# An attention and expert kernel: the issue order of its attention stage rewritten, and the combine's tail product given 128 columns of weights

## The chip, the core and the metric

The kernel runs on one core of one Trainium2 chip. The metric is the device time of one execution in microseconds (us); the kernel before takes 1121.13 us, the median of three runs (1117.65 to 1121.66). The core's engines run side by side and meet through semaphores: TensorE (PE for its matmuls, PEld for its weight loads), VectorE (DVE), ScalarE (ACT), GpSimd (POOL), and SyncE (SP), which here issues DMAs.

## The reference, cut to what matters

```
scores = 0.125 * q @ k.T                        # 4 batches, 8 heads, 576 tokens, 64 wide
keep   = scores >= rowmax(scores) - tau
attn   = softmax(where(keep, scores, -1e9))
x      = (attn @ v) as rows                     # [2304, 512]

logits = x @ w_gate                             # 8 experts, the best one per token
y      = p_best * (relu(x @ w1[e]) @ w2[e])     # e: the token's expert

out    = ((y @ wa) * (y @ wb)) @ wo             # inner width 1536
```

All inputs and the output are float32.

## The kernel before, in words

The work falls into three stages: attention with the gate (to about 415 us), the experts (to about 664 us), and the gated product with the stores of its rows. The change touches the first stage alone.

Attention works on 16 pairs of heads: pair i holds heads p and p+4 of batch i//4, with p = i % 4. A pair has nine score tiles: J, the joint last 64 tokens of both heads; A0 to A3, four blocks of 128 tokens of head a = 0; and B0 to B3 of a = 1. That makes 144 tiles g = 9i, 9i+1, and so on. One tile goes through five units. `s:g` is the score product on PE (line 644), into one of two PSUM buffers. `m:g` is the row maximum on DVE (line 657), `th:g` the threshold for two tiles at once (line 661), `e:g` the exponential on ACT (line 665). `p:g` is mask times exponential on DVE (line 677); it writes the tile P (J for the joint one) and is the last reader of the scores, so it frees the PSUM buffer for `s:g+2`. The units `J`, `C`, `H`, `A0` to `A3` and `B0` to `B3` transpose P on PE (line 752) into PSUM slots tp, tc, th and tj, and units that end in `e` and `l` bring each to SBUF as a high and a low part (pt and half; lines 702 to 717, on ACT, DVE or POOL). `v00` to `v11` are the products with v (line 824).

Ahead of a pair stand the splits of k, q and v into a high and a low part (`kh kl qh ql vh vl`, lines 392 and 406, on POOL from pair 1 on), their transposes on PE (`qk`, lines 432, 456 and 457), and the evacuations (`qe`).

Behind a pair, `x0` and `x1` are the combine for a = 0 and a = 1 (line 840 on): float32 products with the 72 columns W2 turn the transposed output o (64 + 8 columns wide by tokens) into rows, tx; four of them for the blocks of 128 tokens (line 851) and one for the 64 tokens of the tail (line 852). `x0s` and `x0t` scale them into x and xt (lines 857 and 866, DVE). Each float32 product is two passes with a weight load each.

After the last pair of a batch comes its gate (line 916 on): some two dozen small DVE instructions in a chain (sums of the logits L and lt, mx, val, first, oh, then ranks on PE, ex, cum, slot, si, base, g), the scaled rows xg and xh (lines 1004 and 1010), and the scatters. The gates of batches 0, 1 and 2 run amid the tiles of pairs 5, 9 and 13. `l_sel` is a chain of nine small DVE instructions behind the gate of batch 2 (lines 481 to 490) that picks the expert whose first rows are worked on early.

The order of all this is written out by hand: `ORDER` (line 59) is a string of 2713 unit names, and `emit` runs them one by one with the scheduler off. Each engine takes its instructions in that order; what one engine waits for is set by semaphores alone.

Of the kernel before, what the change touches and what calls it, by code (L numbers as in the profile page):

```python
# [23 lines left out]
H = 8  # L24
# [75 lines left out]
e:45 v10:3:2 p:44 qe:6:sk0 A1:4:3 A1:4:2 A1:4:0 A1:4:1 A0e:4 v10:3:3 p:45 s:46 v10:3:4 s:47 m:46 pj:45 A1e:4 A0l:4  # L100
A3:4:3 v10o:3 A3:4:2 A1l:4 A2:4:1 A2:4:0 e:46 z:40 A2:4:2 A2:4:3 A3:4:0 A3:4:1 v11:3:0 m:47 A2e:4 v11:3:1 v11:3:2
A3e:4 v11:3:3 th:47 A2l:4 v11:3:4 J2:4 p:46 e:47 qk:6:q0 H:4:1 s:48 qe:6:k2 A3l:4 H:4:0 H:4:2 v11o:3 qe:6:sk2 p:47
B0:4:1 B0:4:0 B0:4:2 m:48 qe:6:q0 s:49 kh:7 B0:4:3 x1:3 e:48 m:49 kl:7 v00:4:0 B0e:4 x1s:3 H:4:3 v00:4:1 v00:4:2
th:49 L:gate:3 v00:4:3 vh:6 e:49 p:48 qk:6:q1 B0l:4 He:4 p:49 s:50 qe:6:q1 Hl:4 s:51 qh:7 m:50 B1:4:3 B1:4:2 B1:4:0
ql:7 B1:4:1 v00:4:4 m:51 B1e:4 B2:4:0 B2:4:2 B2:4:3 B2:4:1 e:50 B1l:4 vl:6 lk:8 v00o:4 th:51 x1t:3 B3:4:0 p:50 e:51
B3:4:1 B3:4:3 v01:4:0 v01:4:1 v01:4:2 B2e:4 lt:gate:3 p:51 v01:4:3 lv:7 tl:gate:3 v01:4:4 B2l:4 s:52 top:gate:3
v01o:4 s:53 C:5:0 shift:gate:3 B3:4:2 tr:gate:3 m:52 ex:gate:3 v10:4:0 Ce:5 B3e:4 v10:4:1 slot:gate:3 v10:4:2 e:52
J:5:0 B3l:4 J:5:1 J:5:2 J:5:3 base:gate:3 gate:3 g:gate:3 Je:5 qk:7:t m:53 qe:7:kt x0:4 qe:7:t xg1:gate:3 xg2:gate:3
e:53 v10:4:3 qk:7:k0 sc1:gate:3 v10:4:4 xg0:gate:3 qe:7:k0 v10o:4 A0:5:3 sc2:gate:3 xh:gate:3 A0:5:0 A0:5:2 A0:5:1
A0e:5 sc0:gate:3 th:53 Cl:5 p:52 A1:5:1 A1:5:3 A1:5:2 sc4:gate:3 A1:5:0 qk:7:k2 p:53 A1e:5 s:54 qe:7:k2 xg3:gate:3  # L110
A1l:5 s:55 m:54 A2:5:3 A2:5:0 A2:5:2 A2:5:1 m:55 A3:5:1 A3:5:0 e:54 A3:5:2 A3:5:3 sc3:gate:3 qe:7:sk2 v11:4:0 rinv:4
v11:4:1 e:55 v11:4:2 th:55 x0s:4 v11:4:3 p:54 v11:4:4 A2e:5 Jl:5 A3e:5 p:55 s:56 kh:8 x0t:4 s:57 A2l:5 v11o:4 A3l:5
qe:7:sk0 H:5:3 H:5:0 m:56 H:5:1 H:5:2 qk:7:q0 He:5 B0:5:3 m:57 B0:5:1 B0:5:2 B0:5:0 kl:8 e:56 Hl:5 e:57 th:57 x1:4
p:56 pj:54 qe:7:q0 J2:5 p:57 s:58 B0e:5 qk:7:q1 x1s:4 A0l:5 s:59 m:58 qe:7:q1 B1:5:3 B1:5:2 B1:5:0 m:59 B1:5:1 e:58
# [134 lines left out]
class Attention:  # L249
# [1482 lines left out]
```

## Time and profile before

| what | us |
|---|---|
| median of 3 runs | 1121.13 |
| lowest and highest run | 1117.65, 1121.66 |
| the profiled execution | 1126.54 |
| its span | 1124.8 |
| PE busy in the span | 1056.7 |
| DVE busy | 801.7 |
| POOL busy | 686.5 |
| ACT busy | 503.9 |

The profiled execution took 1126.54 us, of which 1124.8 are the span from the first to the last recorded instruction. Its mean granted TensorE clock was 0.98 of 2.4 GHz. Busy time of one engine says nothing yet on what another waits for; for that the stage has to be cut into stretches.

### The profile page before, as it was taken

What the parts mean: (1) busy time and instruction counts of PE and PEld (TensorE: products, weight loads), DVE (VectorE), ACT (ScalarE), POOL (GpSimd) and SP (SyncE); (2) the same over time, 40 slices, a digit from 0 to 9 for tenths busy, and PEclk for the clock granted to TensorE, in tenths of its full rate; (3) what the DMA queues carried; (4) which work ended last, traced back from release to release, by engine and by line L of the source; (5) the groups of instructions that cost most, each with busy time, mean ns of one, the idle gap of its engine ahead of it and who ended that gap; (6) DMA issues with size and microseconds to landing.
All of it is one profiled execution on the core that took longest, in us unless ns stands there. A gap on an engine that the chain in (4) does not pass through costs nothing. (4 is left out here: it accounts for less than half of the span.)

```text
span 1124.8 us, 19277 instructions
## 1 busy us (share of the span) xinstructions
PE 1056.7 (94%) x6492; PEld 947.7 (84%) x6492; DVE 801.7 (71%) x1765; ACT 503.9 (45%) x1047; POOL 686.5 (61%) x720
## 2 busy tenths in 40 slices
PE   3899989989988989999999979999999999999996
PEld 3799889979978979999999968888888888888885
DVE  4888888898888787644445799597496794984212
ACT  3788768867856533333334433442231321322110
POOL 3779798888886646555567846455364563654234
PEclk9899999999989998999999989999999999999999
DMA  4478632233222258545556522121011110110012
GB/s 128 116 208 243 188 97 67 77 96 84 69 75 66 86 160 277 174 147 150 159 162 199 161 65 65 49 74 39 20 57 39 38 56 20 57 39 1 10 66 93
DMA packets 105558, 111.81 MB, mean 99 GB/s; under 512 B 16704, under 2 KB 79168, under 8 KB 105456
## 3 DMA queue, kind: packets, MB, share of 16 engines
q1 hardware_dynamic: 101502, 100.79, 31.0%
q0 software_dynamic: 3552, 9.45, 2.2%
q8 instruction: 53, 0.87, 0.3%
q14 instruction: 49, 0.40, 0.1%
q10 hardware_dynamic: 402, 0.29, 0.1%
HBM read 77.47 MB, written 23.08 MB: 89 GB/s over the span
## 5 line engine op out<-in xcount | busy, mean ns | idle before, releaser
L1621 PE MATMUL pg<-y,w 128*128 128x512 f32 (+1 forms) x1440 | 308.6, 373 | 6.5 <-DVEq L1555 6.5
L1621 PEld LDWEIGHTS pg<-y,w 128*128 128x128 f32 x1440 | 253.0, 189 | 58.4 <-ACTq L1555 6.7
L1631 POOL TENSOR_TENSOR g<-gg,g 128x512 fp32r<-128x512 f32 (+1 forms) x60 | 73.3, 1222 | 138.9 <-ACT g L1630 131.4
L1644 PE MATMUL po<-w,g 128*128 128x512 f32 x648 | 152.7, 391 | 0.0
L1644 PEld LDWEIGHTS po<-w,g 128*128 128x128 f32 x648 | 121.2, 188 | 26.2
L717 POOL TENSOR_TENSOR pt<-st,pt 128x512 fp32r<-128x512 f32 x93 | 119.7, 1289 | 28.7 <-ACT pt L707 17.0
L1455 PE MATMUL ph_i<-xt_i,w 128*128 128x256 f32 (+5 forms) x768 | 124.7, 312 | 2.7 <-ACT w L1367 1.7
L1472 PE MATMUL py_i<-h_i,w 128*128 128x256 f32 (+5 forms) x768 | 119.9, 305 | 3.2 <-DVE h_i L1459 1.9
L1455 PEld LDWEIGHTS ph_i<-xt_i,w 128*128 128x128 f32 x768 | 113.2, 191 | 4.2 <-ACT w L1367 1.9
L1472 PEld LDWEIGHTS py_i<-h_i,w 128*128 128x128 f32 x768 | 111.7, 188 | 4.0 <-DVE h_i L1459 2.3
L1628 DVE TENSOR_TENSOR gg<-ga,pg 128x512 f32<-128x512 f32 (+1 forms) x60 | 37.8, 630 | 103.7 <-PE pg L1621 97.3
L1368 DVE TENSOR_TENSOR w<-raw,w 128x512 fp32r<-128x512 f32 x64 | 63.1, 988 | 60.7 <-ACT w L1367 59.3
L1370 POOL TENSOR_SCALAR w<-raw 128x512 fp32r<-128x512 f32 x64 | 50.9, 797 | 86.5 <-DMA raw<-in_moe_w 57.1
L1630 ACT CAST g<-gg 128x512 fp32r<-128x512 f32 (+1 forms) x60 | 34.6, 576 | 149.2 <-DVE gg L1628 79.6
L1401 POOL TENSOR_TENSOR t<-t,w 128x256 f32<-128x256 f32 x72 | 63.7, 890 | 57.8 <-DVE u L1397 26.5
L824 PE MATMUL pv<-pt,sv 128*128 128x288 f32 x512 | 97.4, 313 | 0.8 <-POOL pt L717 0.6
L1371 POOL TENSOR_TENSOR w<-raw,w 128x512 fp32r<-128x512 f32 x64 | 89.3, 1396 | 4.8
L752 PE MATMUL tp<-idf,P 128*128 128x128 f32 x504 | 82.3, 281 | 4.6 <-ACT pt L707 1.5
L1649 DVE TENSOR_TENSOR acc<-acc,po 128x512 f32<-128x512 f32 x90 | 60.5, 683 | 26.8 <-PE po L1644 26.8
L824 PEld LDWEIGHTS pv<-pt,sv 128*128 128x128 f32 x512 | 74.0, 191 | 2.5 <-POOL pt L717 0.8
L1400 POOL TENSOR_TENSOR mag<-a,u 128x256 f32<-128x256 f32 x72 | 60.6, 842 | 24.2 <-DVE a L1398 24.2
L1391 ACT ACTIVATE mag<-raw 128x256 f32<-128x256 f32 x72 | 31.2, 437 | 95.3 <-DVE w L1402 95.2
(267 smaller groups left out, 2079.4 us busy)
## 6 DMA issues: line engine op xcount, KB each, us to landing
raw<-in_moe_w SPq DMA_DIRECT2D x128, 256.0 KB
xs<-zero SPq DMA_DIRECT2D x16, 768.0 KB
raw<-in_moe_w_a SPq DMA_DIRECT2D x12, 512.0 KB
raw<-in_moe_w_b SPq DMA_DIRECT2D x12, 512.0 KB
raw<-in_moe_w_out SPq DMA_DIRECT2D x12, 512.0 KB
kT<-kT SPq DMA_DIRECT2D x32, 160.0 KB
kT<-kT SPq DMA_DIRECT2D x32, 144.0 KB
raw_k<-in_k SPq DMA_DIRECT2D x16, 256.0 KB
```

The lines of the kernel that those rows point to most:

```text
L717: nc.gpsimd.tensor_sub(lo, st, fr(hi))
L752: nc.tensor.transpose(st["ps"][:, 128 * j:128 * j + 128], parts(j), idf)
L824: nc.tensor.matmul(R["v", n][:, 0:HALF], lhs, rhs[r], start=(c == 0 and r == 0), stop=(c == 4 and r == 1))
L1368: nc.vector.tensor_sub(lo_t, raw, fr(hi_t))
L1371: self.last_pool = nc.gpsimd.tensor_sub(lo_t, raw, fr(hi_t)).ins
L1400: g.tensor_sub(mag, a.bitcast(F32), u.bitcast(F32))
L1401: g.tensor_sub(t, t, fr(hi))
L1455: nc.tensor.matmul(ps[:, 0:n], w[a][:, k, :], xt[b][:, k, 0:n], start=(s_ == 0), stop=(s_ == len(steps) - 1))
L1472: nc.tensor.matmul(st["y"][d][:, 0:n], w[a][:, 0, d * P:d * P + P], h[b][:, 0:n], start=(f == 0 and (a, b) == (0, 0)), stop=(f == 7 and a ...
L1621: nc.tensor.matmul(ps[:, 0:n], w[g][j][m][a][:, k, :], self.y[b][:, k, c0:c0 + n], start=(s_ == 0), stop=(s_ == len(steps) - 1))
L1631: last = nc.gpsimd.tensor_sub(gl[:, 0:n], gt[:, 0:n], fr(gh)[:, 0:n])
L1644: nc.tensor.matmul(ps, res[j][a][:, t * P:t * P + P], w[g][j][2][b][:, 0, :], start=(s_ == 0), stop=(s_ == len(steps) - 1))
```

## The change: a new order, and a wider tail product

There are two edits. The first is the text of `ORDER`: the same 2713 units in another order, so that no unit is added or taken away. The order of the experts and of the gated stage is as it was. One line of the new table, amid the gate of batch 2, against the one nearest to it in the old:

```diff
-v10:12:3 v10:12:4 base:gate:11 gate:11 qe:15:t g:gate:11 x0:12 A0e:13 th:125 xg2:gate:11 xg1:gate:11 qk:15:k0
+g:gate:11 v01:12:1 v01:12:2 e:123 B3l:12 th:123 v01:12:3 xg2:gate:11 v01:12:4 p:122 tr:gate:11 v01o:12 A1:13:3
```

The second is in the combine:

```diff
-            ot = (0, 512)[a]
+            ot = (0, 448)[a]
...
-                nc.tensor.matmul(pv_[64 * a:64 * a + 64, 4, :], o[:, ot:ot + 64], w2, start=True, stop=True)
+                nc.tensor.matmul(pv_[:, 4, :], o[:, ot:ot + 128], w2, start=True, stop=True)
```

The weights of the tail's product are now 128 columns of o instead of 64. For a = 0 they are tokens 0 to 127 of o, whose first 64 are the tail; for a = 1 the last 128, whose last 64 are the tail. The result fills all 128 partitions of its 72 columns, and `x0t` and `x1t` read the same 64 of them as before. Lines behind 841 move down by one.

What the new order moves is shown at three places; the numbers behind names only tell one tile from another.

The first place is the start. On POOL, the splits of q (sq1) and k (sk1) of pair 1, before:

```order
L392 TENSOR_SCALAR sq1_276<-raw_q1_242 128x9x64
L406 TENSOR_TENSOR sq1_276<-raw_q1_242,sq1_276 128x9x64
L392 TENSOR_SCALAR sk1_298<-raw_k1_239 128x9x64
L406 TENSOR_TENSOR sk1_298<-raw_k1_239,sk1_298 128x9x64
L392 TENSOR_SCALAR sk2_364<-raw_k2_303 128x9x64
L406 TENSOR_TENSOR sk2_364<-raw_k2_303,sk2_364 128x9x64
```

and now:

```order
L392 TENSOR_SCALAR sk1_289<-raw_k1_239 128x9x64
L406 TENSOR_TENSOR sk1_289<-raw_k1_239,sk1_289 128x9x64
L392 TENSOR_SCALAR sq1_298<-raw_q1_242 128x9x64
L406 TENSOR_TENSOR sq1_298<-raw_q1_242,sq1_298 128x9x64
L392 TENSOR_SCALAR sk2_358<-raw_k2_304 128x9x64
L406 TENSOR_TENSOR sk2_358<-raw_k2_304,sk2_358 128x9x64
```

The k of pair 1 is split ahead of its q; the four instructions are the same.

On PE at the same place, the transposes of pair 1 (tt1, tq1) and the first score products (S0_J0, S0_A0), before:

```order
L456 MATMUL tt1_313<-idr_67,sq1_276 128x128
L457 MATMUL tt1_313<-idr_67,sk1_298 128x128
L432 MATMUL tq1_316<-idr_67,sq1_276 128x128 x4
L432 MATMUL tq1_324<-idr_67,sq1_276 128x128 x4
L432 MATMUL tq1_330<-idr_67,sk1_298 128x128 x4
L644 MATMUL S0_J0_335<-kT0_267,qj0_245 128x288 x8
```

and now:

```order
L456 MATMUL tt1_313<-idr_67,sq1_298 128x128
L457 MATMUL tt1_313<-idr_67,sk1_289 128x128
L432 MATMUL tq1_317<-idr_67,sk1_289 128x128 x4
L432 MATMUL tq1_322<-idr_67,sq1_298 128x128 x4
L644 MATMUL S0_J0_331<-kT0_273,qj0_245 128x288 x8
L644 MATMUL S0_A0_340<-kT0_273,qT0_276 128x288 x4
```

Two groups of four transposes of pair 1 stand ahead of the first score product instead of three; the other two follow behind S0_A0, where one did before.

The second place is the gate of batch 2, on DVE, amid the tiles B0 to B3 of pair 13 (P13_0 to P13_3 are their `p` units, mt their maxima). Before, the last rows ahead of P13_2; P13_1 stands 13 rows above the first of them:

```order
L985 TENSOR_REDUCE slot_70<-cum2_4761 128x5
L987 CAST si2_4765<-slot_70 128x4
L989 TENSOR_SCALAR si2_4765<-slot_70,role_203 128x1
L993 TENSOR_TENSOR base_71<-base_71,tr2_4749 128x8
L975 TENSOR_REDUCE g2_4780<-ex2_4744 128x5
L976 TENSOR_SCALAR g2_4780<-g2_4780 128x5
L977 RECIPROCAL g2_4780<-g2_4780 128x5
L661 TENSOR_REDUCE m13_B2_4733<-mt2_213 128x2
L1004 TENSOR_SCALAR xg2_4794<-x2_3517,g2_4780 128x512
L1010 TENSOR_SCALAR xh2_4802<-xt2_3518,g2_4780 128x256
L1004 TENSOR_SCALAR xg2_4794<-x2_3517,g2_4780 128x512
L677 SCALAR_TENSOR_TENSOR P13_2_4613,sg1_227<-S13_B2_4694,m13_B2_4733,e13_B2_4759 128x576
```

and now, from P13_0 on:

```order
L677 SCALAR_TENSOR_TENSOR P13_0_4551,sg1_227<-S13_B0_4623,m13_B0_4650,e13_B0_4656 128x576
L983 TENSOR_TENSOR cum2_4728<-tr2_4716,base_71 128x40
L984 TENSOR_TENSOR cum2_4728<-cum2_4728,oh_69 128x40
L986 TENSOR_REDUCE slot_70<-cum2_4728 128x5
L988 CAST si2_4732<-slot_70 128x4
L990 TENSOR_SCALAR si2_4732<-slot_70,role_203 128x1
L677 SCALAR_TENSOR_TENSOR P13_1_4561,sg1_227<-S13_B1_4645,m13_B0_4650,e13_B1_4704 128x576
L994 TENSOR_TENSOR base_71<-base_71,tr2_4716 128x8
L1011 TENSOR_SCALAR xh2_4767<-xt2_3521,g2_4696 128x256
L657 TENSOR_REDUCE mt2_213<-S13_B2_4742 128x1
L657 TENSOR_REDUCE mt2_213<-S13_B3_4770 128x1
L711 TENSOR_TENSOR half1_13_4758<-tc13_4753,half0_13_4757 128x2x64
```

The gate's chain no longer stands in one piece between P13_1 and P13_2: the rows from mx to g stand ahead of P13_0, those from cum to si between P13_0 and P13_1, base and xh behind P13_1.

The third place is `l_sel`, on DVE. Before, it stands between the tiles P14_0 and P14_1 of pair 14:

```order
L677 SCALAR_TENSOR_TENSOR P14_0_4911,sg2_229<-S14_A0_4856,m14_J0_4854,e14_A0_4888 128x576
L711 TENSOR_TENSOR half1_13_4700<-th13_4882,half0_13_4699 128x512
L481 TENSOR_TENSOR l_cnt_4929<-base_71,eb_85 128x8
L483 TENSOR_REDUCE l_mx_4931<-l_cnt_4929 128x1
L484 TENSOR_SCALAR l_cnt_4929<-l_cnt_4929,l_mx_4931 128x8
L485 TENSOR_TENSOR l_cnt_4929<-l_cnt_4929,desc_190 128x8
L486 TENSOR_REDUCE l_mx_4931<-l_cnt_4929 128x1
L487 TENSOR_SCALAR sel_72<-l_cnt_4929,l_mx_4931 128x8
L488 TENSOR_SCALAR kept_73<-l_mx_4931 128x1
L489 TENSOR_SCALAR l_mx_4931<-l_mx_4931 128x1
L490 CAST lead_74<-l_mx_4931 128x1
L657 TENSOR_REDUCE mt4_219<-S14_A1_4913 128x1
```

and now:

```order
L677 SCALAR_TENSOR_TENSOR P13_2_4614,sg1_227<-S13_B2_4742,m13_B2_4788,e13_B2_4812 128x576
L1005 TENSOR_SCALAR xg2_4711<-x2_3520,g2_4696 128x512
L481 TENSOR_TENSOR l_cnt_4845<-base_71,eb_85 128x8
L483 TENSOR_REDUCE l_mx_4847<-l_cnt_4845 128x1
L484 TENSOR_SCALAR l_cnt_4845<-l_cnt_4845,l_mx_4847 128x8
L485 TENSOR_TENSOR l_cnt_4845<-l_cnt_4845,desc_190 128x8
L486 TENSOR_REDUCE l_mx_4847<-l_cnt_4845 128x1
L487 TENSOR_SCALAR sel_72<-l_cnt_4845,l_mx_4847 128x8
L488 TENSOR_SCALAR kept_73<-l_mx_4847 128x1
L489 TENSOR_SCALAR l_mx_4847<-l_mx_4847 128x1
L490 CAST lead_74<-l_mx_4847 128x1
L657 TENSOR_REDUCE mt3_216<-S14_J0_4833 128x1
```

It stands between P13_2 and P13_3 (three rows below the last one shown), directly behind the gate of batch 2.

## Rows read from the trace of the kernel before

**Rows 1.** Busy time by stretch: window, length, busy us of PE, PEld, DVE, ACT, POOL, PEclk, DMA, GB/s

```profile
40.00:130.00 90.00, 87.38 (x675) 81.59 (x673) 79.43 (x184) 73.92 (x147) 72.31 (x79) 0.99 0.74 213
130.00:150.00 20.00, 16.21 (x117) 14.47 (x117) 16.48 (x47) 11.60 (x25) 15.74 (x16) 0.94 0.31 97
...
230.00:250.00 20.00, 16.73 (x127) 14.28 (x126) 17.87 (x47) 14.41 (x29) 17.06 (x20) 1.00 0.29 91
...
315.00:345.00 30.00, 23.38 (x159) 21.26 (x158) 26.14 (x68) 17.16 (x35) 22.02 (x24) 0.84 0.20 64
```

**Rows 2.** Waits of PE, 0 to 430 us: total us, times, longest us

```profile
PE S_A L644 <- DVE P L677: 5.9, 10, 2.2
...
PE S_B L644 <- DVE P L677: 5.1, 10, 1.7
```

**Rows 3.** Timeline, 8 to 21 us: start, us, engine, line, operation, names, [idle before]

```profile
8.96 0.56 SPq L372 DMA_DIRECT2D raw_k<-in_k  x1
...
10.07 0.56 SPq L372 DMA_DIRECT2D raw_q<-in_q  x1
...
14.61 0.67 POOL L392 TENSOR_SCALAR sq<-raw_q 128x576 fp32r<-128x576 f32 x1 [12.20 <-DMA raw_q<-in_q]
...
20.12 0.71 PE L432 MATMUL tq<-idr,sk 128*128 128x128 f32 x4
...
20.62 2.25 PE L644 MATMUL S_J<-kT,qj 128*128 128x288 f32 x8
```

**Rows 4.** Timeline of PE at one combine

```profile
128.78 1.01 PE L851 MATMUL tx<-W,o 128*128 128x72 f32 x8
...
129.72 0.34 PE L852 MATMUL tx<-W,o 128*64 128x72 f32 x2
...
129.99 0.54 PE L824 MATMUL pv<-pt,sv 128*128 128x288 f32 x2
```

**Rows 5.** Weight loads of the combine's products, 0 to 425 us: busy us, mean ns

```profile
L851 PEld LDWEIGHTS tx<-W,o 128*128 128x128 f32 x256 | 32.1, 195 | 3.6 <-issue 2.1 <-DVE half L711 1.1 <-ACT qT L450 0.2
...
L852 PEld LDWEIGHTS tx<-W,o 128*64 128x64 f32 x64 | 6.2, 137 | 2.4
```

**Rows 6.** Timeline of DVE: P around the gates of batches 0, 1, 2

```profile
136.71 0.81 DVE L677 SCALAR_TENSOR_TENSOR P<-S_B,m_B,e_B 128x576 f32<-128x576 f32 x1
...
144.75 0.80 DVE L677 SCALAR_TENSOR_TENSOR P<-S_B,m_B,e_B 128x576 f32<-128x576 f32 x1
...
227.00 0.81 DVE L677 SCALAR_TENSOR_TENSOR P<-S_B,m_B,e_B 128x576 f32<-128x576 f32 x1
...
236.32 0.81 DVE L677 SCALAR_TENSOR_TENSOR P<-S_B,m_B,e_B 128x576 f32<-128x576 f32 x1
...
315.49 0.81 DVE L677 SCALAR_TENSOR_TENSOR P<-S_B,m_B,e_B 128x576 f32<-128x576 f32 x1
...
321.51 0.18 DVE L982 TENSOR_TENSOR cum<-tr,base 128x40 f32<-128x40 f32 x1
...
322.46 0.19 DVE L975 TENSOR_REDUCE g<-ex 128x5 f32<-128x40 f32 x1
...
323.52 0.79 DVE L1010 TENSOR_SCALAR xh<-xt,g 128x256 f32<-128x256 f32 x1
...
325.06 0.80 DVE L677 SCALAR_TENSOR_TENSOR P<-S_B,m_B,e_B 128x576 f32<-128x576 f32 x1
```

**Rows 7.** Groups of DVE, 0 to 425 us: busy us, mean ns

```profile
L711 DVE TENSOR_TENSOR pt<-tp,pt 128x512 fp32r<-128x512 f32 x33 | 22.5, 683 | 0.1
```

**Rows 8.** Timeline of DVE around l_sel

```profile
333.09 0.81 DVE L677 SCALAR_TENSOR_TENSOR P<-S_A,m_J,e_A 128x576 f32<-128x576 f32 x1
...
334.43 0.39 DVE L481 TENSOR_TENSOR l_cnt<-base,eb 128x8 f32<-128x8 f32 x1
...
338.39 1.41 DVE L657 TENSOR_REDUCE mt<-S_A 128x1 f32<-128x576 f32 x2
...
340.25 0.82 DVE L677 SCALAR_TENSOR_TENSOR P<-S_A,m_A,e_A 128x576 f32<-128x576 f32 x1
```

More of the change, by code (lines that the diff above doesn't have):

```diff
@@ L100 @@
[L100 to L114, printed above, removed]
@@ L220 @@
[L220 to L222 removed]
+kh:0 qh:0 ql:0 kl:0 qk:0:t qk:0:q1 qe:0:t qk:0:k2 qe:0:kt qe:0:q1 qk:0:k0 qe:0:k2 qk:0:q0 kh:1 qe:0:k0 qe:0:sk2
+qe:0:q0 kl:1 qe:0:sk0 qh:1 vh:0 vl:0 ql:1 lk:2 lv:1 qk:1:t qe:1:t qk:1:k0 qk:1:q0 qe:1:kt qe:1:k0 s:0 s:1 m:0
@@ new lines @@
+slot:gate:3 Je:5 e:49 x0:4 g:gate:3 th:49 xg3:gate:3 xg2:gate:3 sc3:gate:3 p:48 base:gate:3 gate:3 s:50 xh:gate:3
+xg1:gate:3 p:49 kh:7 m:50 kl:7 A0:5:2 v10:4:0 v10:4:1 A0:5:0 v10:4:2 A0:5:1 s:51 rinv:4 A0:5:3 e:50 m:51 qh:7 A0e:5
+Cl:5 th:51 p:50 v10:4:3 v10:4:4 sc1:gate:3 e:51 A1:5:0 A1:5:2 xg0:gate:3 s:52 sc4:gate:3 v10o:4 A1:5:1 p:51 A1:5:3
+A3:5:0 sc0:gate:3 m:52 A1e:5 A3:5:1 A3:5:2 s:53 x0s:4 e:52 ql:7 A1l:5 A2:5:0 A2:5:2 A2:5:1 m:53 A2:5:3 A3:5:3 A2e:5
+v11:4:0 lk:8 x0t:4 v11:4:1 th:53 qk:7:t e:53 p:52 v11:4:2 v11:4:3 qe:7:t A0l:5 v11:4:4 p:53 s:54 qe:7:kt A3e:5 A2l:5
@@ new lines @@
+lt:gate:7 v00:8:3 m:86 tl:gate:7 B1:8:0 B2:8:3 B2:8:1 B0l:8 B1e:8 B2:8:0 top:gate:7 lv:11 v00:8:4 C:9:0 B2:8:2 e:86
+m:87 v00o:8 J2:8 Ce:9 shift:gate:7 v01:8:0 B2e:8 th:87 v01:8:1 B1l:8 v01:8:2 e:87 B2l:8 tr:gate:7 p:86 v01:8:3
+ex:gate:7 B3:8:3 B3:8:0 B3:8:2 slot:gate:7 B3:8:1 s:88 B3e:8 v01:8:4 base:gate:7 gate:7 p:87 J:9:0 B3l:8 J:9:1
+v01o:8 J:9:3 qk:11:t J:9:2 m:88 s:89 qe:11:t Cl:9 e:88 g:gate:7 x0:8 m:89 xg3:gate:7 qe:11:kt Je:9 xh:gate:7
+xg1:gate:7 qk:11:k0 e:89 v10:8:0 v10:8:1 xg2:gate:7 sc3:gate:7 A0:9:2 A0:9:3 qe:11:k0 A0:9:1 A0:9:0 xg0:gate:7
@@ new lines @@
+xg1:gate:11 v10:12:2 base:gate:11 gate:11 xh:gate:11 qe:15:t s:125 sc1:gate:11 qk:15:k0 qe:15:kt v10:12:3 m:124
+qe:15:k0 v10:12:4 sc4:gate:11 A0:13:1 A0:13:2 A0:13:0 m:125 A0:13:3 v10o:12 x0:12 qe:15:sk0 e:124 Cl:13 sc2:gate:11
+th:125 e:125 A1l:13 A2:13:3 A2:13:0 A2:13:1 A2:13:2 A0e:13 p:124 xg0:gate:11 s:126 sc3:gate:11 l_sel qk:15:k2
+sc0:gate:11 A2e:13 v11:12:0 qe:15:k2 v11:12:1 v11:12:2 m:126 v11:12:3 qe:15:sk2 A3:13:2 A3:13:1 A0l:13 x0s:12
+A3:13:0 v11:12:4 e:126 A3:13:3 x0t:12 p:125 H:13:2 A3e:13 H:13:1 H:13:0 vh:15 A2l:13 H:13:3 s:127 He:13 A3l:13
@@ new lines @@
+x1t:15 L:gate:15 l_wd:5:0 l_wl:5:1 l_ah:1 l_wh:5:1 lt:gate:15 l_ad:1 l_b:0 l_wd:5:1 l_wl:6:0 tl:gate:15 l_ap:2
+top:gate:15 shift:gate:15 tr:gate:15 ex:gate:15 l_wh:6:0 g:gate:15 slot:gate:15 l_ah:2 xg3:gate:15 xg2:gate:15
+sc3:gate:15 l_ad:2 l_b:1 l_ap:3 xg0:gate:15 l_wd:6:0 l_wl:6:1 xg1:gate:15 xh:gate:15 sc0:gate:15 l_ah:3 base:gate:15
+gate:15 sc4:gate:15 l_ad:3 l_b:2 l_ap:4 sc1:gate:15 l_wh:6:1 l_ah:4 sc2:gate:15 l_ad:4 l_b:3 l_ap:5 l_wd:6:1 l_ah:5
+l_ad:5 l_b:4 l_ap:6 l_wl:7:0 l_wh:7:0 l_wd:7:0 l_wl:7:1 l_wh:7:1 l_wd:7:1 l_ah:6 l_ad:6 l_b:5 l_ap:7 l_ah:7 l_ad:7
```

287 lines of the change are left out of this document (140 added, 147 removed).

## The prediction

> **What bounds the kernel now.** I read the table of busy shares first, then busy time by stretch, then PE's waits, then the timeline at the places where PE waits. Over the whole span PE is busy 94% (the table in the section on time and profile), so only two things can move the time: less work for PE, or less idle time of PE. By stretch the second is seen to be uneven. In an undisturbed stretch of attention, 40 to 130 us, PE is busy for 87.38 of 90 us and DVE for 79.43 [rows 1]: PE is the bound there, and DVE has 10.6 us to spare. In the three stretches with a gate PE is busy for 16.21 of 20, 16.73 of 20 and 23.38 of 30 us [rows 1], so it lacks 3.8, 3.3 and 6.6 us; DVE has 16.48, 17.87 and 26.14 there, and in the first two it sits in a chain of small dependent instructions. At the share of the undisturbed stretch (97.1%) the three together would lack 2.0 us in their 70, so 3.8 + 3.3 + 6.6 − 2.0 = 11.7 us of idle time are extra. The third also has a mean granted clock of 0.84 and the first of 0.94 [rows 1]. There are two levels, 2.4 and 1.2 GHz; if the missing share is time at 1.2 GHz, full speed is missed for 0.16 × 30 + 0.06 × 20 = 6.0 us. Extra idle time and clock together are 17.7 us, an upper bound of what the gates cost.
>
> PE's own waits say for what: the score products of A and B tiles wait for a P of DVE 20 times, 5.9 + 5.1 = 11.0 us in all [rows 2]. The reason is in the two PSUM buffers of the scores: P is the last reader, so a gap between two P's on DVE is a gap between two score products on PE, and PE lives through it only on transposes and products with v that are ready by then.
>
> **The start.** POOL waits 12.20 us for raw_q before it splits q of pair 1 at 14.61 [rows 3], and the k of pair 1 is split behind it. The issue of raw_k stands at 8.96, that of raw_q at 10.07 [rows 3]. With k first, POOL can start by the 1.1 us between the two issues earlier, if k lands as much earlier as it is issued; that is an estimate from the issues. PE's transposes of pair 1 wait for both splits, whose sum is the same, so they come 1.1 us earlier. Then one group of four transposes less stands ahead of the first score product: 20.12 to 20.62 is 0.5 us [rows 3]. Everything behind depends on this first score, and PE has nothing else: −1.1 − 0.5 = −1.6 us. Bounds: if both transfers land together, only the 0.5 stays, and if the group that was put off is in the way of S0_A1, nothing; no reason is seen for a loss, but the same four transposes placed later could cost their 0.5 again: +0.5 to −1.7.
>
> **The tail product.** It is issued 32 times, two passes each. Eight passes with 128 columns of weights run from 128.78 to 129.72, 0.94 us, so 0.235 for a product of two; the tail's two passes with 64 columns run from 129.72 to 129.99, 0.27 us [rows 4]. With 128 columns it is one more product like the four before it: 32 × (0.235 − 0.27) = −1.1 us, all of it on PE, which is the bound. What speaks against it is the weight load: the loads take 195 ns with 128 columns, 137 ns with 64 [rows 5]. Each is under the matmul before it as long as that one is longer. If it were not, 64 × 0.058 = +3.7 us would come in place of the gain. I take −1.1, since a product of this very form stands four times next to the one that is replaced; the ends are −1.1 and +3.7. DVE waits for tx afterwards as before.
>
> The Trainium skill has a rule that speaks against this edit: in "TensorE: Matmul & The Clock Gate", section "LDWEIGHTS (loading the stationary operand)", the time of a weight load goes by the number of columns alone, so twice the columns would be twice the load. By it the loads would grow by 64 × 0.137 = 8.8 us and, if nothing hid them, the time to 1121.13 − 1.6 − 4.1 + 8.8 = 1124.2 us. The trace agrees in direction but not in size (195 against 137 ns is 1.42 times, not 2) [rows 5], and it shows that the product with the wider load is no longer one [rows 4].
>
> **The gates.** Before, DVE's gate stands in one lump between two P's. The gaps from P to P are 136.71 to 144.75 = 8.04 us, 227.00 to 236.32 = 9.32 us, and 315.49 to 325.06 = 9.57 us [rows 6]. In the new order P's stand amid the chain (the second excerpt of the order). Priced on batch 2: the rows cum to base leave the long lump, 321.51 to 322.46 = −0.95; xh and the xg behind it leave it too, 323.52 to 325.06 = −1.54 [rows 6]. An evacuation pt (line 711) comes into it, +0.68 [rows 7], and the small sum lt, for which I take the 0.19 of the reduction g [rows 6]. Together −1.6. In batch 1 the same pieces are spread over three gaps, and I take −1.6 as well; in batch 0 xh, the other xg and base fall behind the next P and one pt comes in, −1.54 + 0.68 = −0.9. Sum −4.1 us. I count it in full, because in these gaps PE runs dry: it is idle there beyond the share of the quiet stretch. What is taken out of a lump is work that DVE must still do; it falls among P's where DVE has its 10.6 us in 90 to spare, which is what hides it. The bounds: 0, if the total of DVE over a gate's stretch decides and not its longest lump (17.87 of 20 us is near to that), and −9, half of the 17.7 us, if the split lets PE go on through most of each gate.
>
> **The lead select.** The gap with l_sel runs from the P at 333.09 to the P at 340.25, 7.16 us, of which 334.43 to 338.39 = 3.96 is l_sel itself [rows 8]. In its new place the gap holds the same 3.96 beside an xg, one mt, an x and an xt (third excerpt of the order and the three rows behind it), where it held an evacuation half, two mt and three small rows before; about as much work, so I count 0 for the gap alone. What is different is its place: right behind the gate of batch 2 instead of 8 us later. It is the third rival.
>
> The rest of the order, among quiet tiles, is counted as 0: PE has 97% there, and the new order can neither gain more than the 2.6 us in 90 nor is a reason seen for a loss. The end of attention keeps its chain: last gate, lead expert, first expert weights.
>
> **The sum.** −1.6 − 1.1 − 4.1 = −6.8 us. Against the profiled execution: 1126.54 − 6.8 = 1119.7 us, with 1.7 us of it outside the span as before. That execution stands 5.4 us above the median of the runs (1121.13), so the forecast for the median is 1121.13 − 6.8 = 1114.3 us. Its own range is 1110 to 1118.
>
> **The rivals.** First, the gates stay bound by DVE's total: what is cut from one gap is given back in the next. For it speaks DVE's 17.87 of 20 us in the gate of batch 1; against it, 16.48 of 20 in that of batch 0 [rows 1]. Left are the start and the tail: 1121.13 − 2.7 = 1118.4 us.
>
> Second, the gates lose half of what they cost: −1.6 − 1.1 − 9 = −11.7, 1109.4 us. For it speaks that a chain split among P's leaves no P waiting for more than a few small instructions; against it, that a P is also late when its maximum is.
>
> Third, on the other side: the gate of batch 2 and l_sel become one lump. Before, 8.03 us (325.06 to 333.09) lie between the two gaps [rows 6, 8], in which PE works off what was held up. In the new order only P13_1 and P13_2 lie between them. If PE is dry by then, l_sel's 3.96 us come in full, and PE stays idle long enough to fall to 1.2 GHz once more, which in this stretch costs its 0.16 × 30 = 4.8 us again: +8.8. With the other gates as in the first rival that is 1121.13 − 2.7 + 8.8 = 1127.2 us, 1123 to 1132 by how much of it comes. Against it speaks that xg and the maxima are fewer in this lump. It decides from the point at which the same tiles lose over 8.3 us more than the 6.6 idle and 4.8 of clock they lose now, some 19.7 us.
>
> Fourth, the weight load is not hidden: 1121.13 − 1.6 + 3.7 − 4.1 = 1119.1 us.
>
> **How the numbers follow.** Forecast 0.36, first rival 0.22, second 0.13, third 0.24, fourth 0.05. About 0.5%, or 5.6 us, is what a measurement of this kernel can tell from no change, so faster is below 1115.5 and slower above 1126.7. Faster: 0.30 of the forecast, all of the second, 0.02 of the first: 0.45. Slower: 0.17 of the third and 0.02 for the unknown: 0.19. The same: 0.36. The range is 1105 to 1127: it leaves out about the upper half of the third rival and a little below the second.
>
> **What the profile after would show.** The start is right if the first S_J begins near 19.0 instead of 20.62. The tail is right if its product takes about 0.235 us next to the four others, and wrong if PE's idle time before it grows. The gates are right if the longest gaps between P's fall to about 7 to 8 us and PE's idle time in the three gate stretches falls by about as much; if the gaps fall and the idle time does not, it is the first rival. The third shows as a longer dry stretch of PE from P13_1 to P14_1, with a granted clock of 1.2 GHz over more than 10 us. What would make the whole prediction wrong is a loss in the quiet stretches, with PE under 97%, where I saw no reason for one.

## The result, and the profile after

The changed kernel takes 1111.01 us (median of five runs, 1107.43 to 1112.53); the kernel before, on the same chip, 1121.13 us (1117.65 to 1129.03). The ratio is 0.989, with a 95% interval of 0.987 to 0.991. By the medians that is 10 us less, by the ratio 12, where 6.8 were forecast.

The two profiled executions lie further apart, with spans of 1124.8 and 1105.7 us: the one of before is 5.4 us above its kernel's median, the one of after (1107.43) 3.6 below. About half of the 19 us is thus the luck of two executions, so a single profile is not enough for a gain in time.

Nearly all of it lies ahead of the experts: their first product on PE starts at 414.7 us before and at 396.7 after, 18.0 us apart. For a comparison tile by tile, the stretches below are cut at the masks P of tiles 8, 44, 62, 80, 116 and 143; the gates of batches 0, 1 and 2 lie in the third, fifth and sixth. The windows of the kernel before (length; busy us of PE, PEld, DVE, ACT and POOL; PEclk, the mean granted TensorE clock as a share of 2.4 GHz; DMA share, GB/s; the last line is the whole):

```profile
0.00:41.66 41.66, 19.86 (x114) 18.08 (x115) 23.49 (x88) 18.42 (x37) 19.66 (x34) 0.92 0.46 118
41.66:121.28 79.62, 77.32 (x603) 72.28 (x603) 70.83 (x167) 65.69 (x131) 64.11 (x70) 1.00 0.73 208
121.28:170.41 49.13, 44.15 (x328) 40.37 (x328) 42.33 (x107) 34.51 (x70) 41.98 (x45) 0.97 0.41 124
170.41:211.57 41.16, 39.74 (x313) 37.45 (x313) 36.64 (x86) 34.56 (x68) 35.30 (x39) 1.00 0.26 67
211.57:299.88 88.31, 83.57 (x648) 76.70 (x647) 79.38 (x192) 69.29 (x137) 76.75 (x83) 1.00 0.31 86
299.88:376.03 76.15, 68.03 (x504) 63.49 (x502) 66.90 (x162) 53.52 (x104) 55.55 (x61) 0.93 0.21 64
376.03:414.70 38.67, 35.01 (x273) 33.66 (x272) 30.03 (x105) 12.63 (x28) 21.62 (x21) 0.96 0.48 149
0.00:414.70 414.70, 367.68 (x2768) 342.03 (x2769) 349.60 (x902) 288.62 (x571) 314.97 (x350) 0.97 0.41 117
```

and of the kernel after:

```profile
0.00:37.53 37.53, 17.36 (x117) 15.66 (x117) 23.72 (x88) 18.46 (x37) 19.21 (x34) 1.00 0.46 121
37.53:122.08 84.55, 80.90 (x641) 76.72 (x641) 72.78 (x170) 71.06 (x141) 70.01 (x75) 1.00 0.78 225
122.08:166.19 44.11, 37.89 (x293) 34.41 (x292) 39.71 (x104) 31.44 (x62) 37.68 (x41) 1.00 0.30 90
166.19:204.10 37.91, 37.27 (x301) 35.71 (x300) 35.07 (x83) 32.66 (x66) 33.25 (x36) 1.00 0.32 81
204.10:289.85 85.75, 83.36 (x665) 78.61 (x664) 78.24 (x194) 70.31 (x141) 79.97 (x87) 1.00 0.30 86
289.85:356.87 67.02, 62.68 (x482) 57.45 (x481) 64.20 (x161) 51.47 (x99) 52.19 (x58) 1.00 0.24 73
356.87:396.70 39.83, 34.96 (x282) 33.33 (x281) 30.43 (x103) 13.64 (x31) 24.36 (x24) 1.00 0.42 129
0.00:396.70 396.70, 354.42 (x2769) 331.88 (x2770) 344.14 (x899) 289.02 (x571) 316.67 (x350) 1.00 0.42 121
```

Length less PE's busy time is PE's idle time: 47.0 us before, 42.3 after. Only 4.7 of the 18.0 us are idle time; 13.3 are busy time, though the products are nearly the same. PEclk shows one reason. Before, it is below 1.00 in the first, third, sixth and seventh stretch; its missing shares are 41.66 × 0.08 + 49.13 × 0.03 + 76.15 × 0.07 + 38.67 × 0.04 = 11.7 us at full speed. That is an upper bound of what the clock cost, as part of it falls where PE was idle. After, PEclk is 1.00 in all. The tail's product is the other reason (below).

By stretch: the start, to tile 8, gains 4.1 us, at a PEclk of 1.00 in place of 0.92. Tiles 8 to 80 with the gate of batch 0 gain 3.3 (169.9 to 166.6), and PE's idle time there has grown, from 8.7 to 10.5. Tiles 80 to 116 gain 2.6, tiles 116 to 143 9.1, and the end gives 1.2 back.

What answers to [rows 3], the start after: POOL, and the first score product of PE.

```profile
12.15 0.68 POOL L392 TENSOR_SCALAR sk<-raw_k 128x576 fp32r<-128x576 f32 x1 [9.74 <-DMA raw_k<-in_k]
...
17.74 0.71 PE L432 MATMUL tq<-idr,sq 128*128 128x128 f32 x4
...
18.24 2.25 PE L644 MATMUL S_J<-kT,qj 128*128 128x288 f32 x8
```

S_J begins at 18.24 where I expected some 19.0. To [rows 2], PE's waits for P:

```profile
PE S_B L644 <- DVE P L677: 5.7, 8, 1.5
...
PE S_A L644 <- DVE P L677: 3.1, 4, 1.7
```

8.8 us in place of 11.0. To [rows 6], the P's around the gate of batch 2 on DVE (P13 of A3, then B0 to B3):

```profile
300.09 0.82 DVE L677 SCALAR_TENSOR_TENSOR P<-S_A,m_A,e_A 128x576 f32<-128x576 f32 x1
...
306.68 0.80 DVE L677 SCALAR_TENSOR_TENSOR P<-S_B,m_B,e_B 128x576 f32<-128x576 f32 x1
...
308.62 0.80 DVE L677 SCALAR_TENSOR_TENSOR P<-S_B,m_B,e_B 128x576 f32<-128x576 f32 x1
...
312.28 0.82 DVE L677 SCALAR_TENSOR_TENSOR P<-S_B,m_B,e_B 128x576 f32<-128x576 f32 x1 [0.52 <-ACT e_B L665]
...
317.52 0.80 DVE L677 SCALAR_TENSOR_TENSOR P<-S_B,m_B,e_B 128x576 f32<-128x576 f32 x1
```

The longest gap is 6.6 us instead of 9.57; at the gates of batches 0 and 1 the longest are 6.6 and 6.8 instead of 8.04 and 9.32. To [rows 5], the loads of the combine's weights:

```profile
L852 PEld LDWEIGHTS tx<-W,o 128*128 128x128 f32 x256 | 31.2, 191 | 3.2 <-PE tp L752 1.0 <-ACT js L787 0.9 <-DVE half L711 0.8
...
L853 PEld LDWEIGHTS tx<-W,o 128*128 128x128 f32 x64 | 9.7, 192 | 0.0
```

The tail's loads now take 192 ns like the others, and PEld was never idle before them.

### The profile page after: what moved, and what is told of

It reads as the page before. It is cut to its first block, busy times and chain, and to the rows that moved or that the text cites. A ratio compares the mean times of both kernels' runs of the same rounds, so it can differ in the third digit from the quotient of the medians.

```text
span 1105.7 us, 19292 instructions
## 1 busy us (share of the span) xinstructions
PE 1042.2 (94%) x6492; PEld 936.2 (85%) x6492; DVE 797.0 (72%) x1765; ACT 504.7 (46%) x1047; POOL 688.8 (62%) x720
## 5 line engine op out<-in xcount | busy, mean ns | idle before, releaser
L752 PE MATMUL tp<-idf,P 128*128 128x128 f32 x504 | 86.0, 275 | 3.4 <-ACT pt L707 2.3
L1368 ACT CAST w<-raw 128x512 fp32r<-128x512 f32 x64 | 39.7, 622 | 82.4 <-DMA raw<-in_moe_w 46.3
```

What stands on the lines that cost most here:

```text
L752: nc.tensor.transpose(st["ps"][:, 128 * j:128 * j + 128], parts(j), idf)
```

## The experiments

Each kernel was run against the kernel before on one chip, and ratios are to it; 0.001 is 1.1 us. "Old" and "new" are the order before and after.

| kernel | ratio | 95% interval | us |
|---|---|---|---|
| the change | 0.9890 | 0.9867 to 0.9912 | −12.3 |
| new tail, old order | 0.9979 | 0.9962 to 0.9997 | −2.4 |
| old tail, new order | 0.9893 | 0.9874 to 0.9911 | −12.0 |
| new order to tile 116, new tail | 0.9922 | 0.9902 to 0.9942 | −8.8 |
| new order from tile 117, new tail | 0.9942 | 0.9921 to 0.9963 | −6.5 |
| new order to tile 8 | 1.0002 | 0.9983 to 1.0021 | +0.2 |
| the change, l_sel back | 0.9899 | 0.9873 to 0.9925 | −11.3 |
| old, l_sel early | 0.9970 | 0.9953 to 0.9988 | −3.4 |
| old, gate of batch 2 divided | 1.0022 | 1.0006 to 1.0039 | +2.5 |
| old, base early | 0.9997 | 0.9983 to 1.0011 | −0.3 |
| the change, ql:7 early | 0.9862 | 0.9837 to 0.9888 | −15.5 |
| old, tail of 64 columns twice | 1.0048 | 1.0031 to 1.0065 | +5.4 |
| old, scalings late | 1.0017 | 0.9996 to 1.0038 | +1.9 |

(The us are the ratio less 1, times 1123, about the median of before over these runs.)

**The new tail with the old order.** The diff is the second edit of the change alone.

> The old order with the new tail product alone. My theory (one more product like its four neighbours, 32 times 0.035 us): 1.1 us less than before, 1120.0 us, a ratio of 0.999; in the profile the product's two passes take 0.23 to 0.24 us. The rival (wider weight loads are not hidden): 3.7 us more, 1.003. A second rival, that the tail carries most of the 10 us: a ratio under 0.995.

A combine in the timeline of PE of this kernel (columns as in [rows 4]):

```profile
126.70 1.01 PE L847 MATMUL tx<-W,o 128*128 128x72 f32 x8
127.55 0.39 PE L848 MATMUL tx<-W,o 128*128 128x72 f32 x2
127.73 0.51 PE L819 MATMUL pv<-pt,sv 128*128 128x288 f32 x2
```

From the first of its passes to the instruction behind, the combine now takes 1.03 us; before it took 1.21 [rows 4]. The tail's part went from 0.27 to 0.18, and the four products ahead of it from 0.94 to 0.85. The saving is 0.18 us here and not 0.035. Measured in the same way at all 32 combines, its median is 0.17 and its sum 5.6 us of PE. The whole of attention in this kernel:

```profile
0.00:410.60 410.60, 361.59 (x2769) 340.79 (x2770) 347.80 (x897) 288.60 (x571) 314.29 (x350) 0.97 0.41 117
```

Busy time fell by 367.7 − 361.6 = 6.1 us, and 2.0 came back as idle time (49.0 against 47.0). In time it is −2.4 us, between −0.3 and −4.3: faster, by less than PE was freed. Both rivals, exposed loads and a tail that carries most of the gain, are out.

**The new order with the old tail.** The diff is the table of the change alone.

> The new order with the old tail product. My theory: all but 1.1 us of the gain is the order's, so about 1112 us, a ratio of 0.990 to 0.992. The rival that the order needs the shorter product: a ratio over 0.995.

The order carries nearly the whole change, as expected. Attention in this kernel:

```profile
0.00:400.30 400.30, 361.94 (x2768) 337.21 (x2769) 344.17 (x899) 289.42 (x571) 316.26 (x350) 0.99 0.42 120
```

Against before, idle time falls by 47.0 − 38.4 = 8.6 us and busy time by 5.7, the latter at a granted clock of 0.99 in place of 0.97. With the new tail, busy time falls by 7.5 more and idle time rises by 3.9: in the new order too, part of what the tail frees on PE is idled away. In time the tail is worth 0.3 us in the new order (−12.0 to −12.3), which the intervals do not tell from nothing, nor from the 2.4 us of the old order.

**The order in parts.** Three tables were put together from the old and the new one: a table up to one unit, then the other without the units that were already there. Written as code:

```diff
 # new to tile 116          new to tile 8               new from tile 117
-first, cut, then = old
+first, cut, then = new, "p:116", old
+first, cut, then = new, "p:8", old
+first, cut, then = old, "p:116", new
+head = first[: first.index(cut) + 1]
+ORDER = head + [u for u in then if u not in head]
```

> The new order up to the score mask of tile 116 (the end of pair 12's work on DVE), then the old order for what is left; new tail product. So the start, the gates of batches 0 and 1 and the quiet pairs are new, the gate of batch 2 and l_sel old. Theory A, the gain is the sum of start, tail and single gates: start -1.6 to -2.5, tail -0.8, two gates -2.5: about 1116 us, 0.995. Theory B, half of the gain comes at the gate of batch 2 with l_sel, where the profile of before has the granted clock at 0.84: here nothing of it, about 1116 as well, but then the part behind tile 116 alone gives 5 us more. Theory C, the gain is spread over the quiet stretches: about 9 parts of 12 of 10 us, 1113 us, 0.993.

> The old order up to the score mask of tile 116, then the new one for what is left; new tail product. Only the gate of batch 2, l_sel and the end of attention are new. Theory A (the gates as I summed them, l_sel worth nothing): -1.6 and -0.3 of tail, 1119.2 us, 0.998. Theory B (gate and l_sel together keep PE from running dry and its clock at full): -5 to -8, 1113 to 1116 us, 0.993 to 0.995, with the stretch of pairs 13 and 14 at a granted clock of 1.00. Theory C: about a quarter of 10 us, 1118.6.

> The new order up to the score mask of tile 8 (the first pair), then the old one; old tail product. The start alone. Theory A (1.6 us as summed, passed on in full): 0.9986; with what the profile of after shows (first mask 2.5 us earlier, and no fall of the granted clock between 25 and 50 us): -2.5 to -4.7, 0.996 to 0.998. The rival, that later work takes the lead back: no change, 1.000.

The first two give −8.8 and −6.5 us, with the new tail in both. Less one tail (2.4) they sum to −12.9, near the −12.3 of the change, so the parts add up. Less a tail of 2.4 us each, the order to tile 116 is worth 6.4 us and the rest 4.1, each to within some 3 us. No theory has both numbers: the first part is as large as C had it (−8, where A and B had −5), the second as large as B had it (−5 to −8, where A had −1.9 and C −2.5), with the granted clock at 1.00 in tiles 116 to 143. The start alone is worth nothing that can be measured (−1.9 to +2.4 us), though its profile has the first mask 2.1 us earlier than before.

Where the 6.4 us are made, the profiles show tile by tile, against the kernel with the new tail and the old order. The start takes 2.0 us less. Tiles 8 to 116 take 252.8 in place of 254.9, 2.0 less (with the old tail in both, 254.1 in place of 258.2). Tiles 116 to 143, whose order is the old one in both but for some units that came earlier (491 matmuls instead of 502), take 3.7 less; first with the old order throughout, then with the new order to tile 116:

```profile
295.65:371.69 76.04, 67.23 (x502) 63.49 (x501) 67.81 (x163) 53.75 (x105) 55.30 (x61) 0.93 0.21 65
```

```profile
291.62:363.99 72.37, 64.81 (x491) 60.25 (x489) 65.92 (x162) 52.59 (x103) 54.20 (x61) 0.95 0.22 68
```

The largest single difference there is the gap with l_sel, 7.06 against 5.10 us. The nine rows of l_sel, in their old place in both, sum to 3.82 us in the first and to 1.86 in the second. Why, the next experiment shows.

**l_sel.** In the changed kernel it went back to its old place, in the kernel before to the new one.

```diff
 # the change, l_sel back
-p:124 xg0:gate:11 s:126 sc3:gate:11 l_sel ... p:127 s:128 ... s:129 x1t:12
+p:124 xg0:gate:11 s:126 sc3:gate:11 ... p:127 s:128 ... s:129 l_sel x1t:12
 # old, l_sel early
-p:124 A2:13:1 ... p:127 s:128 ... s:129 l_sel v11:12:4
+p:124 l_sel A2:13:1 ... p:127 s:128 ... s:129 v11:12:4
```

> The changed kernel with l_sel alone moved back to where it was, between the masks P14_0 and P14_1. Theory A (a lump costs by its own length, wherever it stands): no change against the changed kernel, 0.989 of before. Theory P (its new place behind the gate is what saves some 6 us between tiles 127 and 132): 5 to 6 us of the gain go, 0.994 to 0.995, and PE's granted clock falls to 1.2 GHz again near the l_sel. Theory R (my third rival, that next to the gate it makes one long lump): faster than the changed kernel, under 0.987.

> The kernel before with l_sel alone moved: directly behind P13_2, so behind the undivided gate of batch 2. Theory A: no change, 1.000. Theory P: the place alone saves 5 to 6 us, 0.995. Theory R (one lump of the old gate and l_sel): 4 to 8.8 us slower, 1.004 to 1.008, with an idle PE and a granted clock of 1.2 GHz behind P13_2.

In the old order the place alone saves 3.4 us (1.3 to 5.3): theory P in direction, and the opposite of my third rival. In the new order putting it back costs 1 us by the ratios, which the intervals do not tell from nothing: theory A's number fits, and P's 5 to 6 us are not seen. Tiles 116 to 143 of the kernel with l_sel early, and of the change with l_sel back:

```profile
299.54:372.10 72.56, 66.97 (x504) 62.40 (x502) 64.54 (x163) 53.38 (x104) 55.76 (x61) 0.95 0.22 68
```

```profile
292.12:361.37 69.25, 64.01 (x482) 58.93 (x481) 65.58 (x160) 51.88 (x99) 52.05 (x58) 0.98 0.24 71
```

The first is 72.56 us against 76.15 before, the second 69.25 against 67.02 in the change. Before, the longest of the waits in [rows 2] is for the P that ends the gap with l_sel:

```profile
341.13 0.79 PE L644 MATMUL S_A<-kT,qT 128*128 128x288 f32 x4 [2.23 <-DVE P L677]
```

With l_sel early no wait for a P from 300 to 345 us is longer than 0.3. The reason stands in the rows of l_sel itself. Before, with what POOL does at the time (DVE: l_cnt at line 484, line 485, l_mx, sel):

```profile
335.05 0.59 DVE L484 TENSOR_SCALAR l_cnt<-l_cnt,l_mx 128x8 f32<-128x8 f32 x1
...
335.58 2.50 POOL L717 TENSOR_TENSOR pt<-st,pt 128x512 fp32r<-128x512 f32 x2
335.68 1.19 DVE L485 TENSOR_TENSOR l_cnt<-l_cnt,desc 128x8 f32<-128x8 f32 x1
...
336.90 0.16 DVE L486 TENSOR_REDUCE l_mx<-l_cnt 128x1 f32<-128x8 f32 x1
337.10 1.00 DVE L487 TENSOR_SCALAR sel<-l_cnt,l_mx 128x8 f32<-128x8 f32 x1
```

and in the changed kernel, the same four DVE rows:

```profile
314.67 1.00 POOL L42 DMA_INDIRECT xs<-xg,si  x1 [0.17 <-issue]
...
315.10 0.23 DVE L484 TENSOR_SCALAR l_cnt<-l_cnt,l_mx 128x8 f32<-128x8 f32 x1
315.37 0.17 DVE L485 TENSOR_TENSOR l_cnt<-l_cnt,desc 128x8 f32<-128x8 f32 x1
315.57 0.16 DVE L486 TENSOR_REDUCE l_mx<-l_cnt 128x1 f32<-128x8 f32 x1
...
315.76 0.23 DVE L487 TENSOR_SCALAR sel<-l_cnt,l_mx 128x8 f32<-128x8 f32 x1
```

The row with two operands in SBUF takes 1.19 us beside POOL's two-operand pt, and 0.17 beside POOL's scatter; that of sel 1.00 and 0.23. Before, each ends as one of POOL's two pt does: they end at 336.87 and 338.10, and the two pt, 1.25 us each on average from 335.58, at about 336.8 and 338.1. The reduction l_mx takes 0.16 in both. All nine rows of l_sel sum to 3.93 us before, to 1.55 in the change and also 1.56 in the old order with l_sel early. The place counts by what POOL does beside it. Eight profiles have l_sel in its old place and the old order behind tile 116, but for a small edit in three of them. In six of them its rows sum to 3.8 or 3.9 us, and tiles 116 to 143 take 76.0 to 77.5 us. In the other two, the new order to tile 116 and the kernel with base early (below), they sum to 1.86 and 2.90 us, and the tiles take 72.4 and 73.2. In the change with l_sel back they sum to 2.83. The small rows of the three gates (lines 931 to 993, 18 each) sum to 5.67, 5.53 and 6.04 us before, 4.35, 4.69 and 5.52 after. The Trainium skill has a rule for it: in "SBUF — State Buffer", section "SBUF: two separate sides", a DVE instruction with two inputs in SBUF and a GpSimd instruction that reads SBUF take one pair of ports in turn, and the loser stands still for the whole of the other. The row of 1.19 us that began 0.10 us behind POOL's and ended with it, against 0.17, agrees with that.

**The gate of batch 2 divided, in the old order.**

```diff
-ex:gate:11 e:124 slot:gate:11 e:125 ... base:gate:11 ... g:gate:11 x0:12 A0e:13 th:125 ... p:124
+ex:gate:11 e:124 e:125 th:125 p:124 slot:gate:11 ... base:gate:11 ... g:gate:11 x0:12 A0e:13 ...
```

> The kernel before with the gate of batch 2 alone divided: th and the mask P13_2 stand ahead of cum, slot, base, g, xg and xh instead of behind them. Theory A: the gap from P13_1 to P13_2 falls from 9.57 us by 3.0 to 3.5 us, and as PE runs dry there, the time falls by 2 to 3.5 us, 0.997 to 0.998; with the clock kept at 2.4 GHz in this stretch up to 3 us more. The rival (what is cut from one gap comes back in the next, since DVE's total is the bound): the gap falls, the next grows by as much, 1.000.

The P's of P13_1, P13_2 and P13_3 begin at 313.79, 320.18 and 327.13 us. The first gap thus falls from 9.57 to 6.39 us as expected, but the next one, 2.65 us before, is 6.95; tiles 116 to 143 are no shorter,

```profile
298.19:375.07 76.88, 67.82 (x504) 62.97 (x502) 66.86 (x162) 53.55 (x104) 55.63 (x61) 0.93 0.21 64
```

and the time is 2.5 us longer (0.7 to 4.4). The rival holds, and more: this way of dividing the gate, which is not the one of the change, costs time. What PE waits for here is another thing. Its longest wait at this gate is that of the combine of pair 12, before and in this kernel:

```profile
PE tx L851 <- DVE g L975: 1.9, 1, 1.9
```

```profile
PE tx L851 <- DVE g L975: 3.1, 1, 3.1
```

The combine's PSUM slot is the one that the gate's ranks held, and base is its last reader; g, which the profile names, follows base by 0.07 us. What is put ahead of base on DVE, here a P, keeps PE waiting for it.

**base early, in the old order.**

```diff
-shift:gate:11 qe:15:kt tr:gate:11 m:125 ex:gate:11 e:124 slot:gate:11 e:125 ... base:gate:11 gate:11
+qe:15:kt tr:gate:11 slot:gate:11 base:gate:11 gate:11 shift:gate:11 m:125 ex:gate:11 e:124 e:125 ...
```

> The kernel before; at the gate of batch 2 slot and base stand directly behind the ranks, ahead of ex and of the second maximum; nothing else moves. Theory W: what stalls PE at this gate is not a late P but the combine x0 of pair 12, whose PSUM slot is the one of the ranks and comes free with base (in the profile of before PE waits 1.94 us there, in the kernel with the divided gate 3.06 us). Then the wait falls to 0.5 to 1.0 us and the time by 1 us, with the granted clock perhaps up to 3 more. Theory P (the gap between P's counts): the gap stays at 9.6 us and so does the time, 1.000.

The wait did what theory W says:

```profile
PE tx L851 <- DVE ex L955: 0.9, 1, 0.9
```

The time did what theory P says: −0.3 us (−1.9 to +1.2). So the slot is what PE waited for: in all three kernels the wait ends 0.15 us behind the end of base, here at 321.36, long ahead of g (from 321.91). That a wait shorter by 1 us shortens the program is not shown. In its one profile tiles 116 to 143 take 73.2 us, 2.9 less than before, with l_sel's rows at 2.90 us instead of 3.93. That execution is the fastest of its twelve, 1.3 us below their median, and the times do not confirm the gain.

**The tail of 64 columns twice, in the old order.**

```diff
-                nc.tensor.matmul(pv_[64 * a:64 * a + 64, 4, :], o[:, ot:ot + 64], w2, start=True, stop=True)
+                for _ in range(2):
+                    nc.tensor.matmul(pv_[64 * a:64 * a + 64, 4, :], o[:, ot:ot + 64], w2, start=True, stop=True)
```

> The kernel before with the tail's product of 64 columns issued twice in a row. In the profiles the change from 64 to 128 columns shortened the whole combine on PE from 1.21 to 1.05 us, 0.08 at the tail and 0.09 at the four products ahead of it. Theory S (the price is paid once, for going from 128 columns to 64 and back): the second one adds 0.19 to 0.21 us each, 32 times, 6 to 7 us, 1.006. Theory N (a product of 64 columns is dear in itself): it adds 0.27 to 0.35 us each, 9 to 11 us, 1.008 to 1.010.

```profile
88.17 1.01 PE L851 MATMUL tx<-W,o 128*128 128x72 f32 x8
89.11 0.46 PE L853 MATMUL tx<-W,o 128*64 128x72 f32 x4
89.50 0.54 PE L824 MATMUL pv<-pt,sv 128*128 128x288 f32 x2
```

The two tails together take 0.39 us where one took 0.27: the second costs 0.12, less than the 0.19 to 0.21 of theory S. In time it is +5.4 us (3.5 to 7.3), so 0.17 each: S in kind, and N is out. A product of 64 columns by itself is the cheapest of all, 0.12 us against 0.21 with 128 columns (0.85 over four). The combine of 1.21 us is thus 0.85 + 0.12, and 0.24 for going from 128 columns to 64 and back. The narrow product also writes only 64 of the 128 partitions; which of the two PE pays for, no run separates.

**The scalings late, in the old order.** For 25 of the 32 units the edit is of this kind:

```diff
-x1s:2 B1:3:3 B1:3:1 B1:3:0 m:41
+B1:3:3 B1:3:1 B1:3:0 m:41 x1s:2
```

> The kernel before with 25 of the 32 scalings x0s and x1s moved on DVE behind the next maximum, threshold or mask in the table, so that DVE no longer waits in them for the combine (7.3 us in 18 waits before, 0.9 in 3 in the changed kernel). Theory D (these waits are what slows the quiet pairs): 3 to 4 us less, 0.997, and PE idle in tiles 8 to 116 falls by 2 us or more. The rival (DVE has time to spare there): the waits fall to 2 us or less and the time does not, 1.000.

```profile
DVE x L857 <- PE tx L852: 3.7, 12, 0.6
```

The waits fell from 7.3 us in 18 waits to 3.7 in 12, not to 2, and the time did not fall (−0.4 to +4.3): half of these waits went and gave nothing, so theory D's 3 to 4 us are out. The other half is untested.

**One unit more, in the changed kernel.** In the gate of batch 0 PE waits for the split of q of pair 7, which stands behind three scatters on POOL:

```profile
145.45 0.28 PE L456 MATMUL tt<-idr,sq 128*128 128x128 f32 x1 [2.39 <-POOL sq L406]
```

```diff
-qh:7 A0e:5 ... e:52 ql:7 A1l:5
+qh:7 ql:7 A0e:5 ... e:52 A1l:5
```

> The changed kernel with one unit moved: the low part of the split of q of pair 7 (POOL) directly behind the high part, ahead of three scatters of the gate of batch 0. In the profile of the changed kernel PE waits 2.39 us for it at 145.45. If the wait goes and nothing takes its place: 2.4 us faster than the changed kernel, 0.987 of before. The rival (PE has its backlog to work off anyway and waits for the next P instead): no change, 0.989.

```profile
143.30 0.26 PE L456 MATMUL tt<-idr,sq 128*128 128x128 f32 x1 [0.46 <-DVE m_B L661]
...
147.76 0.33 PE L752 MATMUL tp<-idf,P 128*128 128x128 f32 x1 [1.31 <-ACT pt L707]
```

The wait falls to 0.46 us, and a new one of 1.31, for an evacuation, follows. The median is the lowest of all, 1107.95 us, 0.986 of before; its interval overlaps that of the change, so that it beats the kernel before is shown, and that it beats the change is not.

## Why the prediction was right in its direction, and where its steps failed

The time came out in the range, and faster, by 10 us instead of 6.8. That the sum is as near as it is was partly luck: l_sel, which stood at 0, is worth 3.4 us where it was tested alone, the start is not seen in time, and the gates, which were given most, were never tested in the form of the change.

- **The start, −1.6.** The rows came as forecast, and earlier: S_J at 18.24. That "everything behind depends on this first score" and the gain passes in full is not shown: by itself the new start changes the time by +0.2 us (−1.9 to +2.4), an interval that still holds −1.6. In its profile the P of a tile comes 2.7 us earlier than before at tile 9, 2.5 at tile 116 and 1.6 at tile 143.
- **The tail, −1.1.** The sign was right, and the term mis-sized: PE is freed of 5.6 us, −2.4 in time in the old order and −0.3 in the new. The step that failed is "0.94 us, so 0.235 for a product of two": the four products ahead of the tail already carried part of the switch to 64 columns. More idle time of PE ahead of it, which was to show the term wrong, did not come: it is 0.0 before and after.
- **The gates, −4.1.** The step was "What is taken out of a lump is work that DVE must still do; it falls among P's". Dividing one gate by itself, in another way than the change does, cost 2.5 us, and the first rival is right for it. For the gates as the change has them nothing isolates the term, and the profiles speak for it in part. The gaps became 6.6, 6.8 and 6.6 us, and PE's idle time in the stretches of the gates went from 5.0 to 6.2, 4.7 to 2.4 and 8.1 to 4.3 us, 4.9 less in all: more in that of batch 0, where by my own sign the first rival holds; less in that of batch 1; less in that of batch 2, out of which l_sel alone takes 2.5 us of idle time in the old order. Tiles 80 to 116, with the gate of batch 1, take 88.3 us in the old order and 86.5 in the new one with the old tail; tiles 116 to 127, with the gate of batch 2 and without l_sel, 33.2 and 31.8. Both are near the −1.6 that I had, but other units moved in them too.
- **l_sel, 0.** The failing step is "about as much work, so I count 0". Its rows are the same, their durations are not: 3.93 us beside POOL's two-operand work, 1.55 beside its scatters, and −3.4 us of time in the old order. The third rival, one long lump, is refuted by the same run.
- **The quiet tiles, 0.** Without start and tail the new order to tile 116 is worth about 6 us in time. By the profiles 2.0 to 4.1 us lie in tiles 8 to 116, gates of batches 0 and 1 included, whose small rows got 2.2 us shorter; 3.7 come behind tile 116, in an order that hardly changed, 2.0 of them in the gap with the shorter l_sel. So part of what was missed is l_sel again. Tiles 130 to 143, quiet too, take 28.2 us in place of 31.2, of which the end of attention gives 1.2 back.

How much of the gain is clock, the single profiles do not settle: the start of the old order reads a PEclk of 0.92 before and 0.84 in the kernel with the new order from tile 117. The mean granted clock of every run does, in part. Over the 73 runs of the kernel before in the experiments it is 0.982 (0.975 to 0.989), over the five of the change 0.988 (0.986 to 0.991). Among the 73, a run with 0.01 more of it is 4.9 us shorter on average, so the 0.006 between the two kernels go with some 3 of the 12 us. The ten runs of before at 0.987 and above take 1120.4 us on average, still 10 more than the change. So most of the gain is not clock.

Open is which moves in tiles 8 to 116 make their 2 to 4 us, and what each gate of the change is worth by itself. That a shorter l_sel shortens the program is shown in time by one kernel (l_sel early); in the kernel with the new order to tile 116 it is read from one profile.

## What to carry to other kernels

The price of an operation is that of the whole group it stands in: measure from the first instruction of the group to the first one behind it, with and without it, before dividing by the number. Small VectorE instructions cost up to seven times as much beside GpSimd's elementwise work (0.17 us and 1.19), so an order should put them beside what GpSimd only issues. It goes by when the two meet: with the new order to tile 116, l_sel got shorter in a place that was not touched. A gap on one engine is worth cutting only if the wait behind it is the one that ends last; a lone cut in one gate came back in the next gap.

## What the runs showed of the hardware that was not expected

- Going from float32 products with 128 columns of weights to one with 64 and back costs 0.24 us on PE, twice what that product takes by itself (0.12 us). Computing 64 columns for nothing is cheaper: 0.17 us less per combine.
- A DVE instruction on 128 × 8 values took 0.17 us or 1.19, by what POOL did beside it, and a chain of nine 1.55 to 3.93; a reduction on the same values took 0.16 in both cases.
- A profiled execution lies up to 5.4 us from the median of its kernel, and the granted clock in one and the same order differs between them; a gain of 1 to 3 us in one trace (base early) need not be seen in time.
- Over 73 runs of one kernel the mean granted clock lay between 0.975 and 0.989, and with 0.01 more of it a run was 4.9 us shorter on average.
